# One issue order for every block of a gated causal convolution, and two gate taps of the last eight blocks made beside the VectorE chain

## The chip, the cores and the metric

The kernel runs on one core of a Trainium2 chip. The metric is the device time of one execution in microseconds (us), as a median of several runs. Engines are called as the profile calls them: PE (TensorE), DVE (VectorE), ACT (ScalarE), POOL (GpSimd), SP (which only issues DMAs here). Each works through its own instructions in the order in which the program lists them.

## The reference

```python
def reference(**kwargs):
    ...
    x = attn_out          # [8, 4224, 192]: per head (8 heads of 24 channels) a causal
    ...                   # convolution over 7 positions with softmax(weight)
def _moe_ref(x, w_val, conv_w, w_out):
    B, S, D = x.shape
    K = conv_w.shape[0]                                   # 5
    xp = np.concatenate([np.zeros((B, K - 1, D)), x], axis=1)
    for k in range(K):
        gate_pre += conv_w[k][None, None, :] * xp[:, k:k + S, :]
    gate = 1.0 / (1.0 + np.exp(-gate_pre))
    val = x @ w_val                                       # 192 x 192
    return (gate * val @ w_out)                           # 192 x 192
```

All of it is fp32. The kernel makes an fp32 matmul of accuracy enough from three products of rounded parts: a value is cast to a short form (h), the rest (l) is the difference, and h·h, l·h and h·l are summed in PSUM.

## The kernel before

**Tiling.** The eight sequences are two streams of four. The 192 channels are cut in 128 and 64. A tile x1 holds the first 128 channels of both streams side by side ("two halves", index i = 0 in the gate's functions), a tile x2 the other 64 channels of both streams, one stream on each half of the partitions (i = 1). The token axis is cut into 36 blocks n = 0 to 35: two of some 303 columns, six of 448 (n = 2 to 7), twenty-four of 502 (n = 8 to 31), two of 448 (n = 32, 33), one of 500 and one of 188. An instruction on x1 therefore has twice as many elements (1004 for a 502 block) as one on x2.

**First convolution.** `conv_unit` makes one unit of up to four windows: eight matmul records on PE into a PSUM tile pc, one ACT copy pc to e (L321), and, where a head is complete, DMAs from SP that scatter e into x1 and x2 (L350). Units are made for blocks further on: `todo[n]` of them in block n's turn, namely 3, 6, 3, 5, 5, 4, 3, 3 in turns 0 to 7, then 4, 3, 3 over and over up to turn 25, 2 in turns 26 to 31, none afterwards.

**Gate.** For a block, ACT multiplies the first tap into a PSUM tile (`gate_open`, L384: pa for x1, pb for x2), DVE adds four more taps (`gate_taps`, L391, four instructions), ACT takes the sigmoid into g1 or g2 (`gate_close`, L404). There is one buffer of pa and one of pb, so block n+2's open waits for block n+1's close.

**Matmuls of a turn n**, in PE's order: `diagonal` v of n and o of n-1, `main` v of n (two halves v0 and v1, three matmuls each), `columns` v and o (16 records each, plain fp32), `rows` v and o, `main` o of n-1, then the convolution units. DVE multiplies the values by the gate (`gated`: g2 once, g1 in two halves, L504); `split` and `split_gated1/2` make h on ACT (xh, ph) and l on POOL (xl, pl; xl2 and pl2 for the 64-channel part); `project` copies o out of PSUM on ACT (ot).

**PSUM.** All of v2, o2, v0, v1, o0, o1 (in this order in a turn) and then each pc take the next of five buffers of the pool ps. A tile hence waits until the one allocated five places earlier has been read: o1 until DVE's `gated(n, 2)` has read v2; with three units in a turn the next turn's v0 waits for ACT's copy of the first unit and its v1 for that of the second; with four units v1 waits for the copy of the third.

**Order.** The order is written by hand (`manual_schedule`): the engines execute exactly what the calls of the loop at L571 (turns 0 to 3) and of the loop at L604 (turns 4 to 36) list. They differ in where the gate's steps stand: at L604 all four pa taps of block n+1 come before `gated(n, 2)`, block n+1's pa is closed and n+2's opened in the middle of the turn, and all convolution copies come after `split_gated1` and `project`; at L571 one or two pa taps come first, the rest after the gated products, and close and open stand between the first copies of convolution units and the later ones.

Of the kernel before, what the change touches and what calls it, by code (L numbers as in the profile page):

```python
# [7 lines left out]
F32 = mybir.dt.float32  # L8
# [84 lines left out]
BY_POOL, EARLY, AHEAD = 3, 4, 6  # L93
WARM = 11, 5, 14

HEAD = 4

SOON = {2: (0, 2), 3: (1, 3), 4: (3, 5), 5: (5, 8)}

# [2 lines left out]
def kernel(  # L102
# [262 lines left out]
    def views(n, k=KG - 1):  # L365
        g, o, m = STEPS[n]
        b = second(NJS[g])
        x1v = x1s[g][:, : 2 * b].rearrange("p (a t) -> p a t", a=2)
        return x1v[:, :, o + k : o + k + m], x2s[g][:, o + k : o + k + m]
# [5 lines left out]
    def gate_open(n, i):  # L375
        if n >= N:
            return
        m = STEPS[n][2]
        if i == 0:
            acc = ps_g.tile([128, 2, 512], F32, tag="pa", name=f"pa_{n}")[:, :, :m]  # L380
        else:
            acc = ps_h.tile([128, 512], F32, tag="pb", name=f"pb_{n}")[:, :m]
        accs[n, i] = acc
        nc.scalar.mul(acc, views(n, 0)[i], cwt[:, i, 0:1])  # L384

    def gate_taps(n, i, k0=1, k1=KG):
        if n >= N:
            return
        acc = accs[n, i]
        for k in range(k0, k1):  # L390
            nc.vector.scalar_tensor_tensor(  # L391
                out=acc, in0=views(n, k)[i], scalar=cwt[:, i, k : k + 1],
                in1=acc, op0=ALU.mult, op1=ALU.add,
            )

    def gate_close(n, i):
        if n >= N:
            return
        m = STEPS[n][2]
        if i == 0:  # L400
            dst = g1s[n] = gp.tile([128, 2, MB], F32, tag="g1", name=f"g1_{n}")[:, :, :m]
        else:
            dst = g2s[n] = gp.tile([128, MB], F32, tag="g2", name=f"g2_{n}")[:, :m]
        nc.scalar.activation(dst, accs.pop((n, i)), AF.Sigmoid)  # L404
# [35 lines left out]
    def diagonal(what, n):  # L440
        if not ok(n):
            return
        acc = bank(what, n, 2)
        w, _, _, h2, l2 = operands(what, n)
        r = slice(W22, W22 + 128)
        for i, (a, b) in enumerate(parts(w, h2, l2)):
            nc.tensor.matmul(acc, lhsT=a[:, r], rhs=b, start=(i == 0), stop=False)  # L447

    def main(what, n, q):
        if not ok(n):  # L450
            return
        fresh = (what, n, q) not in banks
        acc = bank(what, n, q) if fresh else banks[what, n, q]
        w, h, l, _, _ = operands(what, n)
        r = slice(W11, W11 + 128)
        for i, (a, b) in enumerate(parts(w, h, l)):
            nc.tensor.matmul(  # L457
                acc, lhsT=a[:, r], rhs=b[:, q], start=(fresh and i == 0), stop=(not fresh and i == 2)
            )
# [14 lines left out]
    def columns(what, n):  # L474
        if not ok(n):
            return
        m = STEPS[n][2]
        acc = banks[what, n, 2]
        w = w_val if what == "v" else w_out
        x = views(n)[0] if what == "v" else g1s[n]  # L480
        cuts = [m * i // 4 for i in range(5)]
        for i in range(4):
            c = slice(cuts[i], cuts[i + 1])
            for q, p in enumerate(HALVES):
                nc.tensor.matmul(  # L485
                    acc[p, c], lhsT=w.f[:, W12 : W12 + 64], rhs=x[:, q, c],
                    start=False, stop=(i == 3),
                )

    def split(n):  # L490
        if n >= N:
            return
        x1, x2 = views(n)
        if n == 0:
            xs[n, 2] = split2(sp, "x", n, x2)
        xs[n, 1] = split1(sp, "x", n, x1)
        if n > 0:
            xs[n, 2] = split2(sp, "x", n, x2)

    def gated(n, q):  # L500
        if not ok(n):
            return
        v = g1s[n][:, q] if q < 2 else g2s[n]
        nc.vector.tensor_tensor(out=v, in0=banks.pop(("v", n, q)), in1=v, op=ALU.mult)  # L504

    def split_gated1(n):
        if ok(n):
            pr[n, 1] = split1(pp, "p", n, g1s[n])

    def split_gated2(n):  # L510
        if ok(n):
            pr[n, 2] = split2(pp, "p", n, g2s[n])

    def project(n, q):
        if not ok(n):
            return
        m = STEPS[n][2]
        if n not in ots:
            ots[n] = op.tile([128, 3 * MB], F32, tag="ot", name=f"ot_{n}")
        nc.scalar.copy(ots[n][:, q * m : (q + 1) * m], banks.pop(("o", n, q)))  # L520
        o = 3 * sum(s[2] for s in STEPS[:n])
        if n == LAST:
            nc.sync.dma_start(out[:, o + q * m : o + (q + 1) * m], ots[n][:, q * m : (q + 1) * m])
        elif q == 1:
            nc.sync.dma_start(out[:, o : o + 3 * m], ots[n][:, : 3 * m])
# [9 lines left out]
    def conv(k):  # L535
        for _ in range(k):
            if done[0] < len(units):
                conv_unit(done[0])
                done[0] += 1
# [28 lines left out]
    gate_close(0, 1)  # L568
    gate_open(1, 1)

    for n in range(HEAD):  # L571
        k = 2 if n < 2 else 3
        diagonal("v", n)
        split(n + 1)
        diagonal("o", n - 1)
        main("v", n, 0)
        main("v", n, 1)
        gate_taps(n + 1, 0, 1, k)
        columns("v", n)
        gated(n, 2)  # L580
        columns("o", n - 1)
        split_gated2(n)
        project(n - 1, 2)
        rows("v", n)
        gated(n, 0)
        gated(n, 1)
        rows("o", n - 1)
        main("o", n - 1, 0)
        project(n - 1, 0)
        main("o", n - 1, 1)  # L590
        project(n - 1, 1)
        conv(1)
        split_gated1(n)
        now = todo[n] if n == 0 else todo[n] // 2
        conv(now - 1)
        gate_taps(n + 1, 0, k, KG)
        gate_close(n + 1, 0)
        gate_open(n + 2, 0)
        gate_taps(n + 1, 1)
        conv(todo[n] - now)  # L600
        gate_close(n + 1, 1)
        gate_open(n + 2, 1)

    for n in range(HEAD, N + 1):  # L604
        diagonal("v", n)
        gate_taps(n + 1, 0, 1, 3)
        split(n + 1)
        diagonal("o", n - 1)
        main("v", n, 0)
        main("v", n, 1)  # L610
        gate_taps(n + 1, 0, 3, KG)
        columns("v", n)
        gated(n, 2)
        gate_close(n + 1, 0)
        gate_open(n + 2, 0)
        columns("o", n - 1)
        split_gated2(n)
        project(n - 1, 2)
        rows("v", n)
        gated(n, 0)  # L620
        gated(n, 1)
        rows("o", n - 1)
        split_gated1(n)
        main("o", n - 1, 0)
        gate_taps(n + 1, 1)
        project(n - 1, 0)
        main("o", n - 1, 1)
        project(n - 1, 1)
        conv(todo[n])
        gate_close(n + 1, 1)  # L630
        gate_open(n + 2, 1)

# [90 lines left out]
```

## Time and profile before

| | |
|---|---|
| median of 3 runs | 389.67 us (389.61 to 391.33) |
| the profiled execution's own time | 393.35 us |
| its span | 391.6 us |
| mean granted PE clock in it | 0.991 |
| turns of 502 columns with 3 units, start of `main` v1 to the next | 10.3 us |
| the same with 4 units | 11.1 us |
| turns 27 to 30 (2 units), first gated product to the next | 9.8 us |

The span falls into a head of some 40 us (loads, weights, the first turns), a long even stretch up to about 300 us, a stretch to about 350 us with fewer convolution units, and a tail without any. Matmul records are pipelined and overlap, so the busy share of PE alone doesn't say that it is the limit; the starts of successive records do. Durations of one instruction contain an overlap with the next of about 0.1 us, so for a chain the distances of starts are used.

### The profile page before, as it was taken

The page shows a single profiled execution, that of the slowest core. Times are in us where ns is not written, and L with a number is a line of the kernel's source. Part 1 is how long each engine was busy: PE and PEld are TensorE (multiplying, and loading weights), DVE is VectorE, ACT ScalarE, POOL GpSimd, SP SyncE. Part 2 cuts the span into 40 slices and gives each one's busy share as a digit, 9 for nine tenths or more (in the row PEclk, how much of TensorE's full clock was granted, in tenths as well). Part 3 has the DMA queues.
Part 4 walks back from the last instruction along what each step waited for, and adds up shares of the span by engine and source line. Part 5 has one row for each costly group of instructions (what it writes and reads, how often), then busy time and mean ns, then how long its engine had stood idle before and what let it go on. Part 6 is the DMA issues. An engine that isn't in the chain of part 4 may idle for free.

```text
span 391.6 us, 8620 instructions
## 1 busy us (share of the span) xinstructions
PE 378.0 (97%) x3204; PEld 321.6 (82%) x3204; DVE 342.3 (87%) x424; ACT 323.8 (83%) x525; POOL 254.8 (65%) x177
## 2 busy tenths in 40 slices
PE   8699999999999999999999999999999999999895
PEld 8687988898888888888888888888888787788684
DVE  4669899888998998998999899899899999999970
ACT  7458888988888888888889988888888888887863
POOL 1959765566667665666665666766566676776871
PEclk9969999999999999999999999999999999999999
DMA  8777869998687689778868868758987644333223
GB/s 293 210 195 223 253 214 290 258 239 272 210 251 216 180 260 256 210 217 253 224 194 256 219 185 261 218 178 253 257 226 227 211 160 146 114 135 133 80 106 144
DMA packets 38209, 82.49 MB, mean 211 GB/s; under 512 B 4856, under 2 KB 17528, under 8 KB 38168
## 3 DMA queue, kind: packets, MB, share of 16 engines
q1 hardware_dynamic: 36720, 79.90, 67.6%
q0 software_dynamic: 896, 1.31, 1.4%
q10 hardware_dynamic: 552, 0.73, 0.6%
q8 instruction: 25, 0.41, 0.5%
q14 instruction: 16, 0.13, 0.1%
HBM read 29.34 MB, written 26.00 MB: 141 GB/s over the span
## 4 chain that ended last, share of the span: by engine, by line
PE 72%; DVE 13%; DMA 5%; ACT 4%; issue 3%; SPq 2%; POOL 0%; DVEq 0%; ACTq 0%
PE pc L312 20%; PE o L457 10%; PE v L457 9%; PE v L485 7%; PE v L470 6%; PE o L485 6%; DVE pa L391 6%; PE o L470 5%; PE o L447 5%; PE v L447 4%; DVE pb L391 4%; DVE g L504 3%; DMA x<-e 2%; DMA x<-xw 2%; DMA scr<-wv 1%
## 5 line engine op out<-in xcount | busy, mean ns | idle before, releaser
L391 DVE SCALAR_TENSOR_TENSOR pa<-x,cwt,pa 128x1004 f32<-128x1004 f32 (+5 forms) x144 | 172.9, 1201 | 10.7 <-ACT pa L384 6.8
L413 POOL TENSOR_TENSOR xl<-x,xh 128x1004 fp32r<-128x1004 f32 (+5 forms) x36 | 74.8, 2077 | 73.1 <-ACT xh L412 58.9
L312 PEld LDWEIGHTS pc<-band,x 128*120 128x120 f32 x912 | 103.1, 187 | 7.1 <-issue 3.9
L312 PE MATMUL pc<-band,x 128*120 128x122 f32 x912 | 104.2, 272 | 4.3 <-DMA x<-xw 3.8
L391 DVE SCALAR_TENSOR_TENSOR pb<-x,cwt,pb 128x502 f32<-128x502 f32 (+5 forms) x144 | 102.2, 710 | 3.8
L413 POOL TENSOR_TENSOR pl<-g,ph 128x1004 fp32r<-128x1004 f32 (+5 forms) x36 | 79.4, 2204 | 10.3 <-ACT ph L412 7.7
L504 DVE TENSOR_TENSOR g<-v,g 128x502 f32<-128x502 f32 (+5 forms) x108 | 65.8, 642 | 21.1 <-PE v L470 16.1
L404 ACT ACTIVATE g<-pa 128x1004 f32<-128x1004 f32 (+5 forms) x36 | 34.5, 959 | 38.8 <-DVE pa L391 21.1
L321 ACT COPY e<-pc 120x488 f32<-120x488 f32 x114 | 59.1, 586 | 6.4 <-PE pc L312 6.3
L421 POOL TENSOR_TENSOR pl<-g,ph 128x502 fp32r<-128x502 f32 (+5 forms) x36 | 43.0, 1194 | 32.8 <-ACT ph L420 32.7
L520 ACT COPY ot<-o 128x502 f32<-128x502 f32 (+5 forms) x108 | 56.2, 551 | 3.3 <-PE o L457 2.6
L421 POOL TENSOR_TENSOR xl<-x,xh 128x502 fp32r<-128x502 f32 (+5 forms) x36 | 41.8, 1162 | 0.0
L384 ACT ACTIVATE pa<-x,cwt 128x1004 f32<-128x1004 f32 (+5 forms) x36 | 37.8, 1051 | 4.8 <-DMA x<-e 3.7
L485 PEld LDWEIGHTS v<-x,wvf 128*64 128x64 f32 x576 | 29.1, 136 | 11.8 <-issue 11.4
L485 PE MATMUL v<-x,wvf 128*64 128x125 f32 (+4 forms) x576 | 37.2, 270 | 0.0
L412 ACT CAST ph<-g 128x1004 fp32r<-128x1004 f32 (+5 forms) x36 | 35.1, 976 | 1.5 <-DVE g L504 1.5
L485 PE MATMUL o<-g,wof 128*64 128x125 f32 (+4 forms) x576 | 35.6, 264 | 0.0
L412 ACT CAST xh<-x 128x1004 fp32r<-128x1004 f32 (+5 forms) x36 | 34.6, 961 | 0.0
L485 PEld LDWEIGHTS o<-g,wof 128*64 128x64 f32 x576 | 30.9, 136 | 0.1
L457 PE MATMUL o<-ph,woh 128*128 128x502 f32 (+5 forms) x72 | 30.9, 429 | 0.0
L457 PE MATMUL v<-xh,wvh 128*128 128x502 f32 (+5 forms) x72 | 27.2, 377 | 0.3 <-ACT e L321 0.3
L457 PE MATMUL v<-xh,wvl 128*128 128x502 f32 (+5 forms) x72 | 27.1, 377 | 0.0
(75 smaller groups left out, 573.1 us busy)
## 6 DMA issues: line engine op xcount, KB each, us to landing
x<-xw SPq DMA_DIRECT2D x64, 300.0 KB
out<-ot SPq DMA_DIRECT2D x24, 753.0 KB
x<-e SPq DMA_DIRECT2D x40, 285.9 KB
x<-xw SPq DMA_DIRECT2D x20, 360.0 KB
out<-ot SPq DMA_DIRECT2D x8, 672.0 KB
x<-e SPq DMA_DIRECT2D x32, 141.6 KB
x<-e SPq DMA_DIRECT2D x25, 171.6 KB
x<-e SPq DMA_DIRECT2D x16, 94.4 KB
```

The lines of the kernel that those rows point to most:

```text
L312: nc.tensor.matmul(pc[:M, k * WIN : (k + 1) * WIN], lhsT=xtiles[i][:, c : c + M], rhs=band[:, 4 * q + hi, :], start=True, stop=True,)
L321: nc.scalar.copy(e[:, a : a + w], pc[:M, :w])
L384: nc.scalar.mul(acc, views(n, 0)[i], cwt[:, i, 0:1])
L391: nc.vector.scalar_tensor_tensor(out=acc, in0=views(n, k)[i], scalar=cwt[:, i, k : k + 1], in1=acc, op0=ALU.mult, op1=ALU.add,)
L412: nc.scalar.copy(h, x)
L413: nc.gpsimd.tensor_tensor(out=l, in0=x, in1=h.bitcast(F32), op=ALU.subtract)
L421: nc.gpsimd.tensor_tensor(out=l, in0=x, in1=h.bitcast(F32), op=ALU.subtract)
L457: nc.tensor.matmul(acc, lhsT=a[:, r], rhs=b[:, q], start=(fresh and i == 0), stop=(not fresh and i == 2))
L470: nc.tensor.matmul(acc, lhsT=a[p, r], rhs=b[p], start=(fresh and i == 0), stop=(not fresh and i == 2))
L485: nc.tensor.matmul(acc[p, c], lhsT=w.f[:, W12 : W12 + 64], rhs=x[:, q, c], start=False, stop=(i == 3),)
L504: nc.vector.tensor_tensor(out=v, in0=banks.pop(("v", n, q)), in1=v, op=ALU.mult)
L520: nc.scalar.copy(ots[n][:, q * m : (q + 1) * m], banks.pop(("o", n, q)))
```

## The change

The loop for turns 4 to 36 goes, and the loop of turns 0 to 3 serves all turns. In it a third pa tap stands between `gated(n, 2)` and `gated(n, 0)` (from turn 2 on). For blocks 28 to 35, taps 3 and 4 of x2 are no longer DVE's: ACT multiplies tap 3 into an SBUF tile t; tap 4 is multiplied into a tile u by POOL (blocks 28 to 32) or ACT (33 to 35); POOL adds u to t, behind its two subtractions for xl and xl2; DVE adds t to pb in one instruction instead of two taps.

```diff
-HEAD = 4
+ASIDE, BOTH = 28, 33
...
+    def aside(n):
+        if not ASIDE <= n < N:
+            return
+        m = STEPS[n][2]
+        t, u = asides[n] = [
+            pp.tile([128, MB], F32, tag=k, name=f"{k}_{n}")[:, :m] for k in ("t", "u")
+        ]
+        nc.scalar.mul(t, views(n, 3)[1], cwt[:, 1, 3:4])
+        if n < BOTH:
+            nc.gpsimd.tensor_scalar(
+                out=u, in0=views(n, 4)[1], scalar1=cwt[:, 1, 4:5], scalar2=None, op0=ALU.mult
+            )
+        else:
+            nc.scalar.mul(u, views(n, 4)[1], cwt[:, 1, 4:5])
+
+    def aside_sum(n):
+        if n in asides:
+            t, u = asides[n]
+            nc.gpsimd.tensor_tensor(out=t, in0=t, in1=u, op=ALU.add)
...
+        if i == 1 and n in asides:
+            k1 = 3
...
+        if i == 1 and n in asides:
+            nc.vector.tensor_tensor(out=acc, in0=asides.pop(n)[0], in1=acc, op=ALU.add)
...
-    for n in range(HEAD):
-        k = 2 if n < 2 else 3
+    for n in range(N + 1):
+        k, j = (2, 2) if n < 2 else (3, 4)
+        now = todo[n] if n == 0 else todo[n] // 2
+        aside(n + 1)
         diagonal("v", n)
         split(n + 1)
+        aside_sum(n + 1)
         diagonal("o", n - 1)
         main("v", n, 0)
         main("v", n, 1)
         gate_taps(n + 1, 0, 1, k)
         columns("v", n)
         gated(n, 2)
+        gate_taps(n + 1, 0, k, j)
...
         project(n - 1, 1)
-        conv(1)
+        conv(min(1, now))
         split_gated1(n)
-        now = todo[n] if n == 0 else todo[n] // 2
-        conv(now - 1)
-        gate_taps(n + 1, 0, k, KG)
+        conv(max(0, now - 1))
+        gate_taps(n + 1, 0, j, KG)
         gate_close(n + 1, 0)
         gate_open(n + 2, 0)
         gate_taps(n + 1, 1)
         conv(todo[n] - now)
         gate_close(n + 1, 1)
         gate_open(n + 2, 1)
-
-    for n in range(HEAD, N + 1):
...
```

PE's and SP's rows stand in the same order before and after. What moves, at three places:

ACT, turn 16 (three units, pc_69 to pc_71), before: here a row is line, operation, output and inputs with the block's number in the name.

```order
L404 ACTIVATE g1_17_2387<-pa_17_2272 128x1004
L384 ACTIVATE pa_18_2389<-x1_7_1819,cwt_155 128x2x502
L420 CAST ph2_16_2399<-g2_16_2346 128x502
L520 COPY ot_15_2403<-o_15_2_2364 128x502
L412 CAST ph_16_2421<-g1_16_2270 128x1004
L520 COPY ot_15_2403<-o_15_0_2413 128x502
L520 COPY ot_15_2403<-o_15_1_2414 128x502
L321 COPY e_8_1_2330<-pc_69_2438 120x488
L321 COPY e_8_1_2330<-pc_70_2447 120x488
L321 COPY e_8_1_2330<-pc_71_2456 120x488
L404 ACTIVATE g2_17_2465<-pb_17_2348 128x502
L384 ACTIVATE pb_18_2467<-x2_7_1820,cwt_155 128x502
```

ACT, the same turn, after the change:

```order
L447 CAST ph2_16_2394<-g2_16_2346 128x502
L547 COPY ot_15_2398<-o_15_2_2362 128x502
L547 COPY ot_15_2398<-o_15_0_2408 128x502
L547 COPY ot_15_2398<-o_15_1_2409 128x502
L322 COPY e_8_1_2330<-pc_69_2425 120x488
L439 CAST ph_16_2434<-g1_16_2322 128x1004
L431 ACTIVATE g1_17_2439<-pa_17_2324 128x1004
L385 ACTIVATE pa_18_2441<-x1_7_1806,cwt_155 128x2x502
L322 COPY e_8_1_2330<-pc_70_2447 120x488
L322 COPY e_8_1_2330<-pc_71_2456 120x488
L431 ACTIVATE g2_17_2465<-pb_17_2348 128x502
L385 ACTIVATE pb_18_2467<-x2_7_1807,cwt_155 128x502
```

Three instructions of x1's size (the cast ph, the close g1 and the open pa) now stand between the copy of the first unit and that of the second.

DVE, turn 16, before and then after: pa_17 is the gate of the next block, g2_16 and g1_16 are the gated products of this one.

```order
L391 SCALAR_TENSOR_TENSOR pa_17_2272<-x1_7_1819,cwt_155,pa_17_2272 128x2x502 x4
L504 TENSOR_TENSOR g2_16_2346<-v_16_2_2350,g2_16_2346 128x502
L504 TENSOR_TENSOR g1_16_2270<-v_16_0_2368,g1_16_2270 128x502
L504 TENSOR_TENSOR g1_16_2270<-v_16_1_2372,g1_16_2270 128x502
L391 SCALAR_TENSOR_TENSOR pb_17_2348<-x2_7_1820,cwt_155,pb_17_2348 128x502 x4
```

```order
L416 SCALAR_TENSOR_TENSOR pa_17_2324<-x1_7_1806,cwt_155,pa_17_2324 128x2x502 x2
L531 TENSOR_TENSOR g2_16_2346<-v_16_2_2350,g2_16_2346 128x502
L416 SCALAR_TENSOR_TENSOR pa_17_2324<-x1_7_1806,cwt_155,pa_17_2324 128x2x502
L531 TENSOR_TENSOR g1_16_2322<-v_16_0_2366,g1_16_2322 128x502
L531 TENSOR_TENSOR g1_16_2322<-v_16_1_2370,g1_16_2322 128x502
L416 SCALAR_TENSOR_TENSOR pa_17_2324<-x1_7_1806,cwt_155,pa_17_2324 128x2x502
L416 SCALAR_TENSOR_TENSOR pb_17_2348<-x2_7_1807,cwt_155,pb_17_2348 128x502 x4
```

Two pa taps stand ahead of g2 instead of four; the third fills the place between g2 and g1, and the fourth comes last, so pa's close comes later on ACT as well.

POOL, turns 31 and 32 (blocks 32 and 33 are split there), before and then after:

```order
L413 TENSOR_TENSOR xl_32_4138<-x1_12_3664,xh_32_4137 128x2x448
L421 TENSOR_TENSOR xl2_32_4142<-x2_12_3665,xh2_32_4141 128x448
L421 TENSOR_TENSOR pl2_31_4181<-g2_31_4127,ph2_31_4180 128x502
L413 TENSOR_TENSOR pl_31_4203<-g1_31_4057,ph_31_4202 128x1004
L413 TENSOR_TENSOR xl_33_4245<-x1_12_3664,xh_33_4244 128x2x448
L421 TENSOR_TENSOR xl2_33_4249<-x2_12_3665,xh2_33_4248 128x448
L421 TENSOR_TENSOR pl2_32_4288<-g2_32_4234,ph2_32_4287 128x448
L413 TENSOR_TENSOR pl_32_4310<-g1_32_4168,ph_32_4309 128x2x448
```

```order
L398 TENSOR_SCALAR u_32_4148<-x2_12_3652,cwt_155 128x448
L440 TENSOR_TENSOR xl_32_4156<-x1_12_3651,xh_32_4155 128x2x448
L448 TENSOR_TENSOR xl2_32_4160<-x2_12_3652,xh2_32_4159 128x448
L407 TENSOR_TENSOR t_32_4147<-t_32_4147,u_32_4148 128x448
L448 TENSOR_TENSOR pl2_31_4197<-g2_31_4143,ph2_31_4196 128x502
L440 TENSOR_TENSOR pl_31_4235<-g1_31_4128,ph_31_4234 128x1004
L440 TENSOR_TENSOR xl_33_4267<-x1_12_3651,xh_33_4266 128x2x448
L448 TENSOR_TENSOR xl2_33_4271<-x2_12_3652,xh2_33_4270 128x448
L407 TENSOR_TENSOR t_33_4258<-t_33_4258,u_33_4259 128x448
L448 TENSOR_TENSOR pl2_32_4308<-g2_32_4254,ph2_32_4307 128x448
L440 TENSOR_TENSOR pl_32_4339<-g1_32_4239,ph_32_4338 128x2x448
```

The sum into t stands ahead of pl2, the difference for which PE's `diagonal` o of the next turn waits; u stands ahead of xl.

More of the change, by code (lines that the diff above doesn't have):

```diff
@@ L384, in gate_open @@
         nc.scalar.mul(acc, views(n, 0)[i], cwt[:, i, 0:1])
+    asides = {}
+    def aside(n):
[16 more added lines that the diff above has]
+            nc.gpsimd.tensor_tensor(out=t, in0=t, in1=u, op=ALU.add)
     def gate_taps(n, i, k0=1, k1=KG):
@@ L600 @@
         conv(todo[n] - now)
-        gate_close(n + 1, 1)
-        gate_open(n + 2, 1)
-    for n in range(HEAD, N + 1):
[L605 to L629, printed above, removed]
         gate_close(n + 1, 1)
```

## The prediction

> **What bounds the kernel now.** I read the page first (busy shares, chain of waits), then PE's waits and the timeline.
>
> ```profile
> span 391.6 us, 8620 instructions
> PE 72%; DVE 13%; DMA 5%; ACT 4%; issue 3%; SPq 2%; POOL 0%; DVEq 0%; ACTq 0%
> 220.00:240.00 20.00, 20.00 (x169) 16.80 (x168) 18.85 (x22) 17.44 (x29) 13.12 (x9) 1.00 0.74 214
> 320.00:340.00 20.00, 19.97 (x160) 15.92 (x162) 19.55 (x23) 17.16 (x26) 14.01 (x9) 1.00 0.46 154
> ```
>
> The chain that ended last is 72% PE. The window rows (busy us of PE, PE loads, DVE, ACT, POOL, then the granted clock) show PE without idle time at 220 us; the view of PE's waits has no entry at all between 105 and 300 us, so that stretch is PE's own rate. At 320 us DVE is the fullest engine, 19.55 of 20.
>
> ```profile
> 229.25 2.68 PE L312 MATMUL pc<-band,x 128*120 128x122 f32 x24
> 233.83 0.39 PE L457 MATMUL v<-xh,wvh 128*128 128x502 f32 x1
> 239.53 3.52 PE L312 MATMUL pc<-band,x 128*120 128x122 f32 x32
> 244.95 0.39 PE L457 MATMUL v<-xh,wvh 128*128 128x502 f32 x1
> 310.37 1.85 DVE L504 TENSOR_TENSOR g<-v,g 128x502 f32<-128x502 f32 x3
> 311.11 0.49 PE L470 MATMUL o<-ph,woh 64*128 64x502 f32 x1 [0.47 <-DVE g L504]
> 313.46 1.84 PE L312 MATMUL pc<-band,x 128*120 128x122 f32 x16
> 320.20 1.97 DVE L504 TENSOR_TENSOR g<-v,g 128x502 f32<-128x502 f32 x3
> ```
>
> Timeline rows: start, duration, instruction. In the even stretch, v1 (the second half of `main` v) starts 5.70 us ahead of the units (233.83 to 239.53); from the units to the next v1 it is 4.58 us with three units (24 records) and 5.42 with four. So a turn takes 10.28 or 11.12. Late, with two units, DVE repeats every 9.83 us (310.37 to 320.20), and PE even waits for its first gated product (`rows` o, 0.47).
>
> **The even stretch: the second unit's copy comes too late.** The new order already runs in turns 0 to 3, and turn 2 is its only turn with three units and 448 columns. It shows what it does:
>
> ```profile
> 48.75 2.68 PE L312 MATMUL pc<-band,x 128*120 128x122 f32 x24
> 49.78 0.57 ACT L321 COPY e<-pc 120x488 f32<-120x488 f32 x1 [0.43 <-PE pc L312]
> 50.25 0.94 ACT L412 CAST ph<-g 128x896 fp32r<-128x896 f32 x1
> 51.09 0.92 ACT L404 ACTIVATE g<-pa 128x896 f32<-128x896 f32 x1
> 52.04 1.01 ACT L384 ACTIVATE pa<-x,cwt 128x896 f32<-128x896 f32 x1
> 52.99 1.02 ACT L321 COPY e<-pc 120x488 f32<-120x488 f32 x2
> 52.91 0.36 PE L457 MATMUL v<-xl,wvh 128*128 128x448 f32 x1
> 53.60 0.47 PE L457 MATMUL v<-xh,wvh 128*128 128x448 f32 x1 [0.34 <-ACT e L321]
> ```
>
> The first copy starts 1.03 us after the units; then ACT, without a gap, does ph, the close and the open before the second copy. v1 takes that unit's PSUM buffer, so it starts at 53.60. The record before it starts at 52.91; matmuls of this width follow each other by some 0.2, so v1 was due at 53.11: PE loses **0.49 us**. For 502 columns the three ACT steps are longer:
>
> ```profile
> 226.37 1.01 ACT L404 ACTIVATE g<-pa 128x1004 f32<-128x1004 f32 x1 [1.23 <-DVE pa L391]
> 227.41 1.10 ACT L384 ACTIVATE pa<-x,cwt 128x1004 f32<-128x1004 f32 x1
> 228.46 0.59 ACT L420 CAST ph<-g 128x502 fp32r<-128x502 f32 x1
> 229.42 1.03 ACT L412 CAST ph<-g 128x1004 fp32r<-128x1004 f32 x1
> 230.35 1.06 ACT L520 COPY ot<-o 128x502 f32<-128x502 f32 x2
> ```
>
> Starts to starts: ph 0.93, close 1.04, open 1.05. With the copy's 0.47 (49.78 to 50.25) and 0.61 from the second copy's start to v1 (52.99 to 53.60): 0.47 + 0.93 + 1.04 + 1.05 + 0.61 = 4.10. From the units to v1 that makes 1.03 + 4.10 = 5.13 where PE alone needs 4.58: **0.55 a turn**. With four units two copies go ahead (another 0.47) and v1 needs the third: 5.60 against 5.42, 0.18. Twelve turns of three units (9 to 25) and six of four (8 to 23): 12 x 0.55 + 6 x 0.18 = **+7.7 us**. DVE, which repeats every 9.83 where it alone decides, and POOL with 13.12 of 20 us fit into the longer turns. Nothing is won back there, since PE had no waits.
>
> Turns 4 to 7 have waits today: PE's for the gated product is 0.6 in all between 62 and 105 us, and g2 comes two taps earlier now. Against it stands 0.49 for turn 6, and the same for turn 7. I take **0**, between -1 (0.6 and its followers gone) and +1 (both full).
>
> **Turns 26 to 31: DVE's relief meets a loop.** Two taps less and one addition more save, a block,
>
> ```profile
> L391 DVE SCALAR_TENSOR_TENSOR pb<-x,cwt,pb 128x502 f32<-128x502 f32 x96 | 71.3, 743 | 2.6
> L504 DVE TENSOR_TENSOR g<-v,g 128x502 f32<-128x502 f32 x72 | 46.5, 676 | 12.1 <-PE v L470 11.4 <-PE v L485 0.4
> L384 ACT ACTIVATE pb<-x,cwt 128x502 f32<-128x502 f32 x24 | 16.4, 684 | 0.8
> L421 POOL TENSOR_TENSOR xl<-x,xh 128x502 fp32r<-128x502 f32 x24 | 29.1, 1211 | 0.0
> ```
>
> 2 x 0.743 - 0.676 (the addition by the nearest DVE row, also one PSUM and one SBUF input) = 0.81 us, and ACT gains 0.68. DVE alone would then set 9.0 a turn, and PE, with one unit less than the 10.28 turn (0.84, 5.42 less 4.58), 9.4. But the new order closes a circle: g2, then `rows` o (its PSUM buffer was v2), the units, the first copy, ph, close, open, two pa taps, g2 again. From rows: 0.07 (g2's end 311.04 to 311.11) + 2.35 (to 313.46) + 1.03 + 0.47 + 0.93 + 1.04 + 1.13 (the open's 1.10, and 0.03 to DVE as in turn 3 below, 63.63 to 63.66) + 2.54 (two taps; four take 5.08, 305.29 to 310.37) + 0.67 = **10.23 a turn**, however short pb's taps are: DVE then waits for the open pa, as it did for 0.41 in turn 3.
>
> ```profile
> 62.62 1.01 ACT L384 ACTIVATE pa<-x,cwt 128x896 f32<-128x896 f32 x1
> 63.66 4.73 DVE L391 SCALAR_TENSOR_TENSOR pa<-x,cwt,pa 128x896 f32<-128x896 f32 x4 [0.41 <-ACT pa L384]
> 305.29 5.17 DVE L391 SCALAR_TENSOR_TENSOR pa<-x,cwt,pa 128x1004 f32<-128x1004 f32 x4
> 349.49 0.68 DVE L504 TENSOR_TENSOR g<-v,g 128x502 f32<-128x502 f32 x1
> 308.49 2.15 POOL L413 TENSOR_TENSOR xl<-x,xh 128x1004 fp32r<-128x1004 f32 x1 [1.69 <-ACT xh L412]
> ```
>
> From the first gated product of turn 27 to that of 31, 349.49 - 310.37 = 39.12 becomes 3 x 10.23 + 9.9 (the last with 448-column taps) = 40.6: **+1.5**. u on POOL is not in the trace; between 0 and the two-input 1.21 it fits into the 1.69 that POOL waits before xl, so I take 0.
>
> **The tail: the addition ahead of pl2.**
>
> ```profile
> 362.87 1.15 POOL L421 TENSOR_TENSOR pl<-g,ph 128x448 fp32r<-128x448 f32 x1 [2.04 <-ACT ph L420]
> 364.07 0.47 PE L447 MATMUL o<-pl,woh 128*128 128x448 f32 x1 [0.55 <-POOL pl L421]
> 372.49 0.36 PE L447 MATMUL o<-pl,woh 128*128 128x448 f32 x1
> ```
>
> Count from g2 of block 31 (end 350.17). Today pl2 of 32 lets PE's `diagonal` o go on at 364.07, +13.9. After: `rows` o 0.07, units 2.42, first copy 3.45, ph 3.9, close 4.85, open 5.8, second copy 6.75, pb's close and open to 8.4, t and u on ACT (each a little under the 0.684 above, with 448 columns) to 9.6, xh to 10.5; POOL then xl 2.1 (a little under 2.15), and xl2, the sum and pl2 at the 1.15 of the row above, so PE goes on at 16.3: +2.4 later. There is no unit left whose time covers it. The next turn repeats it: PE 16.3, gated product 19.5, POOL's four steps from xh's end 19.4 to 25.5, today 372.49, +22.3. So **+3.2**; behind it PE sets the end as today.
>
> Sum: 7.7 + 0 + 1.5 + 3.2 = **+12.4** on the profiled execution (393.35 with its span of 391.6; it lies 3.7 above the median). The terms are waits for named instructions, so I add the difference to the median; rounding the thinner terms down a little (0.18 and the tail), 12: 389.67 + 12 = **401.7**.
>
> One row speaks of the clock:
>
> ```profile
> 14.35 5.89 DMA x<-xw
> 18.00:22.00 4.00, 1.63 (x8) 1.66 (x9) 3.06 (x4) 2.17 (x4) 3.98 (x6) 0.67 1.04 278
> 22.00:26.00 4.00, 4.00 (x21) 4.00 (x21) 2.42 (x5) 1.52 (x3) 1.49 (x4) 0.50 0.74 190
> ```
>
> After PE had waited for a load up to 20.2, its granted clock was 0.50 for 4 us. The tail's waits of PE (near 2.9 and 1.7 us) are shorter than that one. The Trainium skill, page "TensorE: Matmul & The Clock Gate", section "HAM oscillation", wants no idle gap over about 3.4 us; by that rule the tail keeps its clock and the sum stands, and a gap only 0.5 longer than I work out would lose it. The trace agrees for the long gap; it has none between 1 and 4 us.
>
> **Rivals.**
> 1. *The front loses, the end wins.* The circle is looser than its rows (g2 soon enough for `rows` o) and pl2 isn't late: turns 27 to 30 then go at PE's 9.4 (4 x 0.4 = 1.6 gained), the tail gains DVE's 0.8 three times (2.4). 7.7 - 4.0 = +3.7: 393.4. For: the tail is DVE's today. Against: the circle holds no instruction that the change shortens. 11%.
> 2. *Faster.* One mechanism: the second copy in time. If ACT gets from first to second copy's end within 4.58 - 1.03 = 3.55 us, not 4.10, the front costs nothing, and rival 1's 4.0 and the 0.6 of turns 4 to 7 come in: 385.1. Against: turn 2 needed 3.82 for narrower tiles. 8%.
> 3. *No change.* The front costs half (ACT's starts 0.25 closer, four-unit turns free: 12 x 0.3 = 3.6) and the end gains as in rival 1: 389.3. 7%.
> 4. *The clock falls in the tail.* If one of the two waits is long enough to halve it, 4 us at 0.50 cost 2 more: 403.7. For: the 0.50 after the long wait; against: both are shorter. 12%.
>
> **How the numbers follow.** My sum 62%, the rivals 11, 8, 7 and 12. Slower are my sum and rivals 1 and 4, 85%; within 0.5% (about what a measurement of this kernel can tell from no change) 7%; faster 8%. The sum's own bounds: -1 to +1 for turns 4 to 7, 0.1 a turn either way in the front (1.8), 0 to +5 for the tail; all low gives 396.1, all high 406.7. The range reaches down to 392.5 for rival 1 and up to 406, past rival 4; outside are rivals 2 and 3, 15%, and the last of the high corner.
>
> **What would show it.** In the changed profile: PE waits "v L457 <- ACT e" in nearly every turn of 8 to 25, about 0.35 to 0.55 each, with turns of 10.8 and 11.3; DVE waits for "ACT pa" late; turns 27 to 30 at 10.2; PE waits for "POOL pl" after 360 us. Wrong if v1 waits for nothing in the front, or if the late turns go below 9.8.

## The result, and the profile after

The changed kernel takes **405.23 us** (median of 6 runs, 403.15 to 406.27). The kernel before, run beside it on the same chip, takes 390.51 us (389.61 to 393.47). The ratio is 1.0357 (95% interval 1.0312 to 1.0403): slower by 14.7 us, where 12 were forecast, with the time inside the range and near its upper end.

The page of the changed kernel, its span and the shares of the chain that ended last:

```profile
span 403.4 us, 8629 instructions
PE 46%; ACT 24%; DMA 8%; POOL 8%; issue 7%; DVE 3%; SPq 3%; POOLq 0%; ACTq 0%; DVEq 0%
```

PE's share of the chain fell from 72% to 46%, and ACT's rose from 4% to 24%: where the chain used to run along PE, it now goes through ACT. The same two windows as before (stretch, length, then busy us of PE, PE loads, DVE, ACT and POOL, granted clock, DMA share, GB/s):

```profile
220.00:240.00 20.00, 19.25 (x150) 15.43 (x150) 17.47 (x21) 16.64 (x27) 13.12 (x8) 1.00 0.68 207
320.00:340.00 20.00, 18.89 (x156) 14.99 (x154) 16.89 (x20) 18.25 (x28) 18.80 (x13) 1.00 0.44 149
```

In the even stretch PE has gaps that it did not have (20.00 before). Late, DVE falls from 19.55 to 16.89 of 20, as its relief should make it, while POOL rises from 14.01 to 18.80; and PE does less in the same 20 us. No engine is full there. The waits of the changed kernel (engine, line, what it waited for: us in all, times, longest) say what stands between them:

```profile
DVE pa L416 <- ACT pa L385: 41.1, 33, 2.9
...
PE v L484 <- ACT e L322: 5.7, 15, 0.4
...
PE o L474 <- POOL pl L448: 4.8, 6, 1.4
```

In the kernel before, DVE's wait for an opened pa was a sixth of that, and the list of PE's waits had nothing in the even stretch:

```profile
DVE pa L391 <- ACT pa L384: 6.8, 3, 3.3
```

Where the time went is best read from the starts of the units' matmuls (the pc records of PE), which stand once in every turn, and at the end from the starts of the gated product g2 on DVE. In us, each from one profiled execution:

| | before | after | difference | forecast |
|---|---|---|---|---|
| units of turn 2 to those of turn 8 | 48.75 to 112.51: 63.76 | 47.30 to 111.11: 63.81 | +0.05 | 0 |
| units of turn 8 to those of turn 26 | to 303.09: 190.58 | to 310.64: 199.53 | +8.95 | +7.7 |
| units of turn 26 to g2 of block 31 | to 349.49: 46.40 | to 358.34: 47.70 | +1.30 | +1.5 |
| g2 of block 31 to g2 of block 34 | to 375.62: 26.13 | to 387.51: 29.17 | +3.04 | +3.2 |
| g2 of block 34 to the span's end | 15.98 | 15.89 | -0.1 | 0 |

The rows together give 13.3, which lies within the interval of the ratio (12.2 to 15.7 us); the other 1.4 us between the medians is placed in no stretch. The spans differ by 11.8 only, because turn 2 began at 48.75 in the profiled execution of before, 1.45 later than in the other; the kernels below, with the same loads, began it between 45.2 and 47.8.

Now the even stretch, PE of the changed kernel in one turn of three units and one of four (start, duration, instruction; in brackets the idle time and what ended it):

```profile
233.21 2.68 PE L313 MATMUL pc<-band,x 128*120 128x122 f32 x24
...
237.34 0.38 PE L484 MATMUL v<-xh,wvl 128*128 128x502 f32 x1
237.56 0.38 PE L484 MATMUL v<-xl,wvh 128*128 128x502 f32 x1
238.33 0.50 PE L484 MATMUL v<-xh,wvh 128*128 128x502 f32 x1 [0.39 <-ACT e L322]
238.67 0.39 PE L484 MATMUL v<-xh,wvl 128*128 128x502 f32 x1
...
244.13 3.52 PE L313 MATMUL pc<-band,x 128*120 128x122 f32 x32
...
249.72 0.49 PE L484 MATMUL v<-xh,wvh 128*128 128x502 f32 x1
...
255.54 2.68 PE L313 MATMUL pc<-band,x 128*120 128x122 f32 x24
```

v1 starts 5.12 after the units (238.33 less 233.21; worked out: 5.13). Its neighbours follow each other by 0.22, this one by 0.77: 0.55 lost. But the record behind it comes 0.34 later, not 0.22, so from v1 to the next units it takes 5.80, where it took 5.70. A turn is 10.92 instead of some 10.3. With four units v1 comes 5.59 after them (worked out: 5.60), and 5.82 follow; the list of waits has nothing for these turns, whose loss of 0.17 shows only in the starts. ACT in the same turn:

```profile
234.25 0.56 ACT L322 COPY e<-pc 120x488 f32<-120x488 f32 x1 [0.26 <-PE pc L313]
234.71 1.03 ACT L439 CAST ph<-g 128x1004 fp32r<-128x1004 f32 x1
235.64 1.01 ACT L431 ACTIVATE g<-pa 128x1004 f32<-128x1004 f32 x1
236.68 1.10 ACT L385 ACTIVATE pa<-x,cwt 128x1004 f32<-128x1004 f32 x1
237.72 1.02 ACT L322 COPY e<-pc 120x488 f32<-120x488 f32 x2
```

From the first copy to the second it takes 3.47, with no idle time: ph, close and open, as the order lists them. v1 follows 0.61 behind the second copy's start.

POOL late in the changed kernel:

```profile
336.82 1.56 POOL L398 TENSOR_SCALAR u<-x,cwt 128x502 f32<-128x502 f32 x1
339.10 2.16 POOL L440 TENSOR_TENSOR xl<-x,xh 128x1004 fp32r<-128x1004 f32 x1 [0.73 <-ACT xh L439]
...
342.26 1.24 POOL L407 TENSOR_TENSOR t<-t,u 128x502 f32<-128x502 f32 x1
343.47 1.26 POOL L448 TENSOR_TENSOR pl<-g,ph 128x502 fp32r<-128x502 f32 x1
```

Its six steps and the wait for xh make up the whole turn, and PE waits for its pl2 in turns 28 to 31 by 0.42 to 0.68, and by more in the tail:

```profile
324.48 0.50 PE L474 MATMUL o<-pl,woh 128*128 128x502 f32 x1 [0.68 <-POOL pl L448]
...
375.40 0.47 PE L474 MATMUL o<-pl,woh 128*128 128x448 f32 x1 [1.31 <-POOL pl L448]
384.55 0.47 PE L474 MATMUL o<-pl,woh 128*128 128x448 f32 x1 [1.40 <-POOL pl L448]
```

Two theories are left to tell apart, and a third joins them. **A**: the order makes the loss, by two waits: the late copy of the second unit, and the circle from g2 over `rows` o, the units, the first copy, ph, close and open back to g2. **B**: the circle is an artefact of the sum, and POOL, nearly full, sets the late turns. **C**: the products beside the chain are sound in themselves, and only their place in the queues of ACT and POOL costs.

### The profile page after: what moved, and what is told of

Same layout as the page of the kernel before. It is cut to its first block, busy times and chain, and to the rows that moved or that the text cites. A ratio compares the mean times of both kernels' runs of the same rounds, so it can differ in the third digit from the quotient of the medians.

```text
span 403.4 us, 8629 instructions
## 1 busy us (share of the span) xinstructions
PE 381.2 (95%) x3204; PEld 316.1 (78%) x3204; DVE 332.3 (82%) x416; ACT 334.3 (83%) x536; POOL 269.9 (67%) x190
## 3 DMA queue, kind: packets, MB, share of 16 engines
q0 software_dynamic: 896, 1.31, 1.4%
## 4 chain that ended last, share of the span: by engine, by line
PE 46%; ACT 24%; DMA 8%; POOL 8%; issue 7%; DVE 3%; SPq 3%; POOLq 0%; ACTq 0%; DVEq 0%
PE o L484 9%; PE pc L313 9%; ACT g L431 7%; PE v L484 6%; PE v L512 6%; ACT e L322 6%; PE o L512 5%; PE v L497 5%; DMA x<-e 5%; ACT pa L385 5%; ACT ph L439 4%; PE o L497 4%; SPq L351 3%; DMA x<-xw 3%; POOL xl L440 2%
## 5 line engine op out<-in xcount | busy, mean ns | idle before, releaser
L313 PEld LDWEIGHTS pc<-band,x 128*120 128x120 f32 x912 | 102.0, 185 | 7.3 <-issue 3.6
L416 DVE SCALAR_TENSOR_TENSOR pb<-x,cwt,pb 128x502 f32<-128x502 f32 (+4 forms) x128 | 91.3, 713 | 3.2
L547 ACT COPY ot<-o 128x502 f32<-128x502 f32 (+5 forms) x108 | 59.1, 549 | 40.9 <-PE o L484 37.6
L322 ACT COPY e<-pc 120x488 f32<-120x488 f32 x114 | 60.8, 563 | 12.5 <-PE pc L313 12.4
L512 PEld LDWEIGHTS v<-x,wvf 128*64 128x64 f32 x576 | 29.1, 136 | 11.8 <-issue 11.4
L484 PE MATMUL v<-xh,wvh 128*128 128x502 f32 (+5 forms) x72 | 29.5, 410 | 5.8 <-ACT e L322 5.7
L484 PE MATMUL o<-pl,woh 128*128 128x502 f32 (+5 forms) x72 | 27.2, 378 | 0.4 <-POOL pl L440 0.4
```

Of the source, the lines that this page charges most:

```text
L313: nc.tensor.matmul(pc[:M, k * WIN : (k + 1) * WIN], lhsT=xtiles[i][:, c : c + M], rhs=band[:, 4 * q + hi, :], start=True, stop=True,)
L322: nc.scalar.copy(e[:, a : a + w], pc[:M, :w])
L416: nc.vector.scalar_tensor_tensor(out=acc, in0=views(n, k)[i], scalar=cwt[:, i, k : k + 1], in1=acc, op0=ALU.mult, op1=ALU.add,)
L484: nc.tensor.matmul(acc, lhsT=a[:, r], rhs=b[:, q], start=(fresh and i == 0), stop=(not fresh and i == 2))
L512: nc.tensor.matmul(acc[p, c], lhsT=w.f[:, W12 : W12 + 64], rhs=x[:, q, c], start=False, stop=(i == 3),)
```

## Experiments

The stretches are those of the table above. The last column is the ratio to the kernel before, run on the same chip (there its median was between 390.5 and 391.2).

| kernel | turns 2-7 | 8-25 | 26 to g2 of 31 | tail | median | ratio |
|---|---|---|---|---|---|---|
| before | 63.76 | 190.58 | 46.40 | 26.13 | 390.51 | |
| after | 63.81 | 199.53 | 47.70 | 29.17 | 405.23 | 1.0357 |
| 1 order only | 63.81 | 199.36 | 47.51 | 26.97 | 400.76 | 1.0289 |
| 2 products only | 63.75 | 190.65 | 45.53 | 27.43 | 391.66 | 1.0028 |
| 3 one copy more ahead | 63.37 | 196.09 | 47.70 | 29.22 | 400.88 | 1.0266 |
| 4 sum behind | 63.84 | 199.41 | 47.52 | 28.50 | 402.73 | 1.0322 |
| 5 as 3, one tap ahead | 62.24 | 191.78 | 47.01 | 29.61 | 396.17 | 1.0143 |
| 6 old order, products in 32 to 35 | 63.78 | 190.64 | 46.37 | 26.55 | 391.34 | 1.0022 |
| 7 all copies ahead | 66.76 | 203.91 | 49.84 | 29.20 | 416.05 | 1.0659 |
| 8 casts first | 64.18 | 199.49 | 47.48 | 27.56 | 403.7 | 1.0315 |
| 9 casts first, sum behind | 63.84 | 199.59 | 47.52 | 26.34 | 401.33 | 1.0261 |
| 10 old order, products in 32, 33 | 63.76 | 190.65 | 46.39 | 25.34 | 390.86 | 0.9992 |
| 11 old order, products in 28 to 33 | 63.78 | 190.58 | 44.69 | 25.74 | 388.25 | 0.9959 |

### 1. The order without the products beside

```diff
-ASIDE, BOTH = 28, 33
+ASIDE, BOTH = 36, 36
```

> The changed kernel without the taps made aside: all four x2 taps stay on DVE in every block; only the order of the loop is new. Theory A (the order costs; late turns are held by the circle gated product, rows o, units, first copy, ph, close, open, two taps): the front loses the same 7 to 8 us, turns 27 to 30 stay at 10.2 us although POOL has two instructions less, and only the tail's wait for pl2 goes: about 400 us. Rival B (late turns are held by POOL, which is busy 18.9 of 20 us there): turns 27 to 30 fall to 9.8, about 398. Rival C (the taps made aside cost most of it, the order little): below 394.

Measured: 400.76 us, ratio 1.0289 (1.0245 to 1.0332). The order alone makes 10.25 of the 14.7 us. PE's waits in this kernel, and its units in a late turn:

```profile
PE v L484 <- ACT e L322: 5.7, 15, 0.4
PE o L497 <- DVE g L531: 2.8, 7, 0.9
...
PE o L474 <- POOL pl L448: 0.4, 2, 0.2
```

```profile
318.75 1.84 PE L313 MATMUL pc<-band,x 128*120 128x122 f32 x16
...
328.95 1.84 PE L313 MATMUL pc<-band,x 128*120 128x122 f32 x16
```

The wait for the copy is the same to the tenth. Late, POOL has neither u nor the sum, PE waits for g2 and hardly for pl, and a turn still takes 10.20 (318.75 to 328.95). So the length is there without POOL's new work, and theory B is not needed for it. Whether POOL would hold these turns without the circle is another question, which run 5 bears on.

### 2. The products beside, in the old order

The two loops of before, with these calls in both:

```diff
     for n in range(HEAD, N + 1):
+        aside(n + 1)
         diagonal("v", n)
         gate_taps(n + 1, 0, 1, 3)
         split(n + 1)
+        aside_sum(n + 1)
```

> The two loops of before, with the taps of blocks 28 to 35 made aside as in the change (t on ACT, u on POOL or ACT at the start of the turn, the sum behind POOL's two subtractions). Theory A: main v1 waits for no copy, turns of 10.3 and 11.1 as before; late turns 9.7 to 9.8 (POOL needs some 9.7 with u at 1.55), the tail gains up to 0.8 a turn from DVE: 386 to 389. Rival C (the taps made aside cost): 394 or more, with PE waiting for pl2 as in the changed kernel.

Measured: 391.66 us, ratio 1.0028 (1.0003 to 1.0053): a miss, since a gain was expected. From the units of turn 26 to g2 of 31 it does gain 0.9 us, but the tail loses 1.3. ACT and DVE of this kernel in turn 32, and PE at the start of turn 33:

```profile
355.15 0.65 ACT L403 ACTIVATE u<-x,cwt 128x448 f32<-128x448 f32 x1
355.71 0.93 ACT L440 CAST xh<-x 128x896 fp32r<-128x896 f32 x1
```

```profile
361.10 0.63 DVE L422 TENSOR_TENSOR pb<-t,pb 128x448 f32<-128x448 f32 x1 [1.00 <-POOL t L408]
```

```profile
362.21 0.47 PE L475 MATMUL o<-pl,woh 128*128 128x448 f32 x1 [1.13 <-POOL pl L449]
```

xh starts only when t and u are done; POOL's xl, xl2 and sum follow it; DVE, relieved of two taps, waits 1.00 for the sum, and PE 1.13 for pl2. That is what theory C says, and runs 6 and 8 to 11 follow it up.

### 3. One more copy ahead of close and open

```diff
-        now = todo[n] if n == 0 else todo[n] // 2
+        now = todo[n] if n == 0 else (todo[n] + 1) // 2
```

> The changed kernel with half of the units rounded up, so that in turns of three units two copies, not one, stand ahead of the close and the open. Theory F alone (the second copy's lateness is all that holds the turns of three units): main v1 waits for no copy there, turns fall from 10.9 to 10.3, 12 x 0.6 = 7 us less: 398. Theory A with the circle: the second copy lengthens the way from the gated product through ph, close and open to the next taps by 0.47, 10.23 + 0.47 = 10.7 a turn, so only 0.2 x 12 = 2.5 us come back: 402.7, and PE then waits for DVE's gated product in rows o instead of for the copy in main v1.

Measured: 400.88 us, ratio 1.0266 (1.0241 to 1.0291). PE's waits for a copy are gone from the list, and three-unit turns go from 10.92 to 10.65, not to 10.3. PE in one of them, with one weight load (PEld):

```profile
235.04 0.39 PE L484 MATMUL v<-xh,wvh 128*128 128x502 f32 x1
...
238.48 0.78 PE L497 MATMUL o<-ph,woh 64*128 64x502 f32 x2
...
238.76 0.18 PEld L497 LDWEIGHTS o<-ph,woh 64*128 64x128 f32 x1 [0.32 <-DVE g L531]
...
241.13 3.52 PE L313 MATMUL pc<-band,x 128*120 128x122 f32 x32
```

v1 is in time, but the first two records of `rows` o take 0.78 together for 0.39: the weight load of the second, which writes o1, has waited 0.32 for g2. From v1 to the units it takes 6.09 for 5.70. The wait removed gives way to the next: the circle, into which the second copy has now moved. The late copy of the changed kernel hid it in the even stretch.

### 4. The sum behind the l part

```diff
         split(n + 1)
-        aside_sum(n + 1)
...
         split_gated2(n)
+        aside_sum(n + 1)
```

> The changed kernel with POOL's sum into t behind pl2 instead of ahead of it. If pl2's lateness is what the tail pays: PE's waits for POOL pl in diagonal o shrink by 1.1 each in the tail, 2 to 3 us less in all: 402.5. Late turns 27 to 30: theory A keeps 10.2 (the circle stays, PE then waits for DVE's gated product in rows o); rival B (POOL's own work, 9.7 with u at 1.55, and its wait for xh) lets them fall below 10. If the place of the sum doesn't matter, 405.

Measured: 402.73 us, ratio 1.0322 (1.0291 to 1.0353). The late turns come down to 10.2, but the tail only from 29.17 to 28.50, because the wait changes its place:

```profile
PE v L474 <- POOL xl L448: 3.3, 3, 1.4
...
PE o L474 <- POOL pl L448: 0.4, 2, 0.2
```

PE hardly waits for pl2 any more but for xl2, which is late on its own: t and u still stand ahead of xh.

### 5. One copy more ahead, and one tap less ahead of g2

```diff
-        k, j = (2, 2) if n < 2 else (3, 4)
-        now = todo[n] if n == 0 else todo[n] // 2
+        k, j = (2, 2) if n < 2 else (3, 4) if n < 4 else (2, 4)
+        now = todo[n] if n == 0 else (todo[n] + 1) // 2
```

> As the run with one more copy ahead (400.88 us), and from block 4 on only one pa tap, not two, stands ahead of the gated product of the 64-channel part. Theory A (circle: rows o, units, first copies, ph, close, open, pa taps, gated product, rows o): one tap less takes 1.27 us out of the circle; turns of three units then go from 10.65 to PE's own 10.3 (12 turns, -4.2 us), four-unit turns stay at 11.4 because the third copy is still behind close and open, the late turns go from 10.2 to 9.8; together about 396.4 us. Rival: the taps ahead of the gated product don't matter, since only the late copy does; then as the run with one more copy ahead, 10.65 a turn and 401 us.

Measured: 396.17 us, ratio 1.0143 (1.0111 to 1.0176). PE in a turn of four units and one of three:

```profile
236.36 3.52 PE L313 MATMUL pc<-band,x 128*120 128x122 f32 x32
...
241.96 0.49 PE L484 MATMUL v<-xh,wvh 128*128 128x502 f32 x1
...
247.77 2.68 PE L313 MATMUL pc<-band,x 128*120 128x122 f32 x24
...
252.35 0.39 PE L484 MATMUL v<-xh,wvh 128*128 128x502 f32 x1
...
258.03 2.68 PE L313 MATMUL pc<-band,x 128*120 128x122 f32 x24
```

The four-unit turn takes 11.41, as in the changed kernel (v1 waits for the third copy, 5.60 after the units). The three-unit turn is at PE's own pace again: v1 4.58 after the units, and the next units 10.26 after the last. So in the even stretch both waits of theory A have to go for a turn of three units to get its old length, and with both gone it has it. The late turns are a miss: 9.8 was expected, but from the units of turn 27 to those of turn 31 a turn takes 10.3 in the mean (309.66 to 350.98), no less than in the changed kernel (320.82 to 361.88). With the circle shortened PE waits for POOL there, by up to 1.35 in one turn (the line holds the waits of the tail too):

```profile
PE o L474 <- POOL pl L448: 5.6, 7, 1.4
```

So the way over POOL to pl2 can hold late turns as long as the circle does, and theory B may be right as far as that. What makes pl2 late here was not separated: POOL's own work, xh, for which POOL waits 1.21 in one of these turns, or the second tap that this run puts between g2 and g1. That the total still met the expected 396.4 is partly luck: turns 2 to 7 gained 1.1 us over run 3 that had not been worked out. The tail, where neither wait matters, stays at 29.6.

### 6. The old order, the products in the last four blocks, behind the casts

In the kernel before, both products on ACT:

```diff
     for n in range(HEAD, N + 1):
         diagonal("v", n)
         gate_taps(n + 1, 0, 1, 3)
         split(n + 1)
+        aside(n + 1)
+        aside_sum(n + 1)
```

> The kernel before with its own two loops; taps 3 and 4 of x2 are made aside in blocks 32 to 35 only, both on ACT and behind the casts xh and xh2, with the sum behind xl2. Theory: where DVE sets the turn (31 to 33) it loses 0.77 us a turn and nothing stands ahead of xh any more, so the three turns gain up to 2.3 us: 388 to 388.5 us, ratio 0.995. Rival: PE's rows wait for the l parts (pl, xl) anyway and the sum still stands ahead of pl2; then as the run with the products beside alone, 391 to 392 us.

Measured: 391.34 us, ratio 1.0022 (1.0001 to 1.0043): a miss. From g2 of 31 to that of 33 it takes 18.28 (19.08 before), but the next turn gives it back. DVE and PE of this kernel there:

```profile
368.82 0.68 DVE L422 TENSOR_TENSOR pb<-t,pb 128x500 f32<-128x500 f32 x1 [1.07 <-POOL t L408]
```

```profile
369.94 0.48 PE L475 MATMUL o<-pl,woh 128*128 128x448 f32 x1 [1.23 <-POOL pl L449]
```

In turn 33, xl and xl2 of block 34 and the sum for it stand ahead of pl2 of block 33 on POOL, and DVE and PE both wait. (The expectation of run 10 below calls it the l part of 32; the rows are those of 33.)

### 7. All copies ahead of close and open

```diff
-        now = todo[n] if n == 0 else todo[n] // 2
+        now = todo[n]
```

> The changed kernel with all copies of convolution units ahead of ph, close and open of the wide gate. Theory A (circle): PE never waits for a copy, but each copy more ahead of close and open lengthens the circle by 0.5 us: three-unit turns about 11.2, four-unit turns 11.8, late turns 10.7; about 411 us, slower than the changed kernel. Rival: the late copy alone cost the time of the front; then turns of 10.3 and 11.1 and about 398 us.

Measured: 416.05 us, ratio 1.0659 (1.0617 to 1.0702). No wait of PE for a copy is left, and the kernel is some 11 us slower than the changed one. PE's largest wait, then PE's rows in two turns of three units:

```profile
PE o L497 <- DVE g L531: 10.1, 28, 0.8
```

```profile
227.20 2.68 PE L313 MATMUL pc<-band,x 128*120 128x122 f32 x24
...
238.31 2.68 PE L313 MATMUL pc<-band,x 128*120 128x122 f32 x24
```

Units to units 11.11 (worked out: 11.2): the circle in the open, in the even stretch. The total came out 4 to 5 us above the expectation, of which 2.95 lie in turns 2 to 7, where five and six units stand in a turn and the expectation had counted nothing.

### 8 and 9. The casts first, in the changed kernel

In run 8, ACT's products are taken out of `aside` (POOL's u stays in it) and stand behind xh and xh2:

```diff
         split(n + 1)
+        aside_act(n + 1)
         aside_sum(n + 1)
```

> The changed kernel (405.2 us), but ACT's multiplies (t, and u where ACT makes it) stand behind the casts xh and xh2 and no longer ahead of them; POOL's u stays where it was. Theory: in the tail (blocks 33 to 35) the two multiplies ahead of xh, 1.2 to 1.3 us, are what makes xl, and behind it the sum and the l part that PE waits for, late; from the gated product of block 31 to that of 34 it takes 29.2 us in the changed kernel and would take about 27.5; the late turns get 0.1 or less shorter because the circle of 10.2 us stays: about 403.3 us. Rival: the sum's place ahead of the l part alone is the cost; then 29.2 stays and the time is 405.

In run 9 the sum stands behind pl2 as well:

```diff
         split(n + 1)
+        aside_act(n + 1)
-        aside_sum(n + 1)
...
         split_gated2(n)
+        aside_sum(n + 1)
```

> As the run with the casts first, and POOL's sum into t stands behind the l part of the 64-channel product too. Theory: both steps ahead of PE's l part are gone; the tail from the gated product of block 31 to that of 34 falls to about 26.9 us, that of the order alone, and the late turns to 10.2: about 401 us, the 400.8 of the order alone. Rival: as in the run with the sum behind alone (402.7), because DVE's addition then waits for the sum.

Measured: 403.7 us, ratio 1.0315 (1.0280 to 1.0350), and 401.33, ratio 1.0261 (1.0230 to 1.0293). The tail goes from 29.17 to 27.56 and then to 26.34, close to the 27.5 and 26.9 worked out; the stretch ahead of it goes from 47.70 to 47.5 in both. PE's waits of run 8, then of run 9:

```profile
PE o L479 <- POOL pl L453: 2.7, 2, 1.4
```

```profile
PE o L479 <- POOL pl L453: 0.4, 2, 0.2
```

Taken in this order, the products' place on ACT costs 1.6 us in the tail and 0.2 ahead of it, and the sum's place ahead of pl2 another 1.2. The 0.2 goes as well when only the sum is moved (47.52 in run 4), so it takes both places together to make it. With both mended, the tail is shorter than with the order alone (26.97): the products help there.

### 10 and 11. What is left as a gain, in the old order

Run 10 is run 6 with blocks 34 and 35 left as they were (the second part of the diff). Run 11 makes the products in blocks 28 to 31 as well (the first part), with u on POOL ahead of xl there and t behind the casts as in run 8:

```diff
-ASIDE, BOTH = 32, 32
+ASIDE, BOTH = 28, 32
...
-        if not ASIDE <= n < N:
+        if not ASIDE <= n < 34:
```

> The kernel before with its own two loops and the products beside in blocks 32 and 33 only (both on ACT behind the casts). In the run with blocks 32 to 35 the gated product went from block 31 to 33 in 18.3 us, 0.8 less than in the kernel before, and lost 1.2 from 33 to 34, where the sum for block 34 stood ahead of the l part of 32. Theory: the 0.8 stays and the loss goes: ratio 0.998, 390.0 us beside 390.8. Rival: nothing is left of it, since PE waits for the l part of block 31 instead: ratio 1.000 to 1.002.

> The kernel before with its own two loops; the products beside in blocks 28 to 33 (u on POOL up to block 31, on ACT in 32 and 33; t behind the casts). From the run with the products beside alone comes a gain of 0.9 us in turns 26 to 30 (48.6 for 49.5), from the run with two blocks one of 0.8 in the tail (25.3 for 26.1). Theory: both add up, 1.7 us, ratio 0.996. Rival: the two-block run's gain did not show in its median (0.9992), since what DVE saves is lost again where PE waits for the l part; then 0.998 to 1.001.

Measured: 390.86 us, ratio 0.9992 (0.9972 to 1.0013), and 388.25, ratio 0.9959 (0.9934 to 0.9984). The tail of run 10 is 25.34, 0.8 shorter, as worked out, but its median can't be told from that of before. In run 11 the units of turn 31 come 48.17 after those of turn 26, as near to the 48.6 expected as the tail's 25.74 is to 25.3; in the table's stretches the gain is 1.7 up to g2 of 31 and 0.4 in the tail, 2.1 together, as the medians have it (388.25 beside 390.46). It is the one version here that is faster than the kernel before, by 0.2 to 0.7%.

## Why the prediction was right

**The front, +7.7 forecast, +8.95 measured.** The mechanism is shown: v1 waits for the second unit's copy behind ph, close and open, by 0.55 where 0.55 was worked out (238.33 against a due 237.78), and for the third copy in four-unit turns. The term was mis-sized by what follows the wait: the first record of v1 takes 0.34 to the next instead of 0.22, 0.1 in each of 18 turns. (In turns of three units 0.04 of it doesn't show, because those of before last 10.32 in the mean, not the 10.28 that was read from one.) Turns of three and four units so cost 0.60 and 0.28 in the mean (10.926 for 10.323, 11.403 for 11.118) where 0.55 and 0.18 stood: 12 x 0.60 + 6 x 0.28 = 8.9. What the prediction did not see is that the circle of its late turns lies close behind in the front too: run 3 shows it as soon as the copy is in time.

**Turns 4 to 7, 0 forecast.** +0.05 from turn 2 to turn 8. It is a balance, as the two bounds of -1 and +1 had it: from the units of turn 3 to those of turn 4 the new order gains 1.07 (11.19 for 12.26), and from turn 5 to turn 8 it loses 1.09 (31.30 for 30.21). That the two cancel to 0.05 is luck.

**Turns 26 to 31, +1.5 forecast.** From g2 of 27 to g2 of 31 it takes 40.61 (317.73 to 358.34) where 40.6 stood, 1.49 more than before; from the units of turn 26 on it is +1.30. The circle was worked out as 10.23 a turn, and the order alone has 10.2 (run 1) and makes 1.1 of it. The other 0.2 is one turn of 10.37, and comes from two steps that the prediction did not count in these turns: ACT's product t ahead of xh, and POOL's sum ahead of pl2. PE then waits for pl2; with t behind the casts the 0.2 goes (run 8), and with the sum behind pl2 too (run 4). The prediction put u into POOL's wait ahead of xl, which held, but did not count xh coming later there. So the agreement of 40.61 with 40.6 is closer than the account deserves: the circle alone was put 0.2 too long over these four turns (40.41 in run 1, 315.67 to 356.08), and the wait for pl2 filled that in. Whether the circle alone holds these turns stays open: in the changed kernel PE waits in them for pl2 four times, and for g2 only once.

**The tail, +3.2 forecast, +3.04 measured.** The path is shown: PE's `diagonal` o goes on at 375.40 and 384.55, which is 16.39 and 25.54 behind the end of g2 of block 31 (359.01), where 16.3 and 25.5 were worked out. In the first of the two, errors cancel: xh ends 0.35 later than worked out (10.85 for 10.5), and POOL's four steps behind it are 0.3 shorter (5.5 for 5.8). t and u ahead of xh were counted with 1.2 and the sum with 1.15, ahead of pl2. Taken away one after the other they give 1.61 and 1.22 (runs 8 and 9). The order alone costs 0.84 there (run 1), and the relief of DVE gives back 0.63 when nothing stands in its way (26.97 to 26.34). Taking away the sum's place alone gives only 0.67 (run 4), since xl2 was late as well: the two lie partly beside each other.

**The rivals.** The first wanted a looser circle and a tail that gains; runs 1 and 7 show the circle at its length, and the tail lost. The second and third needed the second copy in time or half as late; it was as late as worked out. The fourth wanted the clock to fall in the tail. The windows of the changed kernel at its end:

```profile
380.00:390.00 10.00, 8.43 (x66) 6.23 (x65) 7.57 (x12) 6.72 (x13) 9.65 (x9) 1.00 0.17 69
...
399.00:403.40 4.40, 0.69 (x4) 0.52 (x4) 0.00 (x0) 0.63 (x2) 0.14 (x1) 0.66 0.49 183
```

The row of 360 to 380 us, with the wait of 1.31, has 1.00 too. So in the tail the clock stays at 1.00 through waits of 1.31 and 1.40 (with the waits for xl2 in the same turns, 2.4 and 1.6, where 2.9 and 1.7 had been worked out) and falls only when PE has nothing left to do. The Trainium skill (page "TensorE: Matmul & The Clock Gate", section "HAM oscillation") wants no idle gap of PE above some 3.4 us. The waits of the tail are shorter, so the trace agrees with that.

**The total.** The sum was 12.4 and the stretches give 13.3: the front's term was 1.25 too small, those of the late turns and the tail 0.2 too large each. Rounding the sum down to 12 went the wrong way. From 401.7 to 405.23 it is 3.5 us: 0.8 because the kernel before took 390.51 in the runs beside it and not the 389.67 that was added to, 0.4 the rounding, 0.9 the terms, and 1.4 that lies between the profiled executions and the medians and is placed nowhere.

## What to carry to other kernels

When buffers of one pool pass from a stage to the next, an instruction that is moved ahead of a copy delays the matmul that takes over the copy's buffer: list, for every buffer, who must read it before the next user, and count what stands ahead of that reader in its own queue. A removed wait shows the next one only if that is looked for: add up the circle through all engines back to the same instruction, and compare it with the length of a turn. Work taken off a full engine goes behind what other engines wait for (here the casts and the l part); ahead of it, it can cost more than it saves, as in the tail of run 2, or give away part of the gain, as in its late turns (0.9, where run 11, with t behind the casts, gains 1.7).

## What the runs showed of the hardware that was not expected

Here a one-input product on POOL (a tile times one number for each partition) takes longer than a two-input sum of the same shape. The groups of the changed kernel (count, then busy us and mean ns of one, and the idle time before them):

```profile
L398 POOL TENSOR_SCALAR u<-x,cwt 128x502 f32<-128x502 f32 x4 | 6.2, 1556 | 0.0
L407 POOL TENSOR_TENSOR t<-t,u 128x502 f32<-128x502 f32 x4 | 5.1, 1264 | 0.0
```

1.56 us against 1.26, outside the bound of 0 to 1.21 that the prediction had taken for it; it cost nothing only because POOL then still waited for xh, 0.42 to 1.40 in the five turns. And a v1 that followed a wait took 0.34 us to the next record instead of 0.22, which is not in the idle time that the view of waits gives (0.39 for a v1 that came 0.55 late). What the 0.34 is due to is not shown: in the kernel before, the first record of `main` o behind `rows` o takes 0.33 to the next (238.07 to 238.40) without a listed wait.
